# Whole gates behind every second attention chunk, and one pair of PSUM banks for two chunks' results

## The chip, the cores and the metric

The kernel runs on one core of a Trainium2 chip. The metric is the device time in microseconds (us) of one execution. TensorE (PE) multiplies matrices, VectorE (DVE) and ScalarE (ACT) work elementwise, GpSimd (POOL) works elementwise too and issues transfers, SyncE (SP) issues transfers. Matmul results land in PSUM, which has 8 banks of 2 KB per partition.

## The reference

Three layers in float32, one behind the other. First a linear attention with a decaying state, over 4 batches, 8 heads, 768 positions, head size 64; then two feed-forward layers over all 3072 tokens:

```
state = gamma * state + outer(k[t], v[t])
y[t]  = scale * q[t] @ state
x = y as (3072, 512)
x = (((x @ w1) * (x @ w2)) @ w3) @ w_out            # 512 -> 1024 -> 1024 -> 512
h = x @ w_in;  out = (h * sigmoid(1.702 h)) @ w_out2 # 512 -> 2048 -> 512
```

The five weight matrices come as 64-bit numbers.

## The kernel before

Each operand of a large product is split into a high and a low part (`wh`, `wl`, `xh`, `xl`), and a product is three matmuls: wh·xh, wh·xl, wl·xh (`mm3`, L258 to L260). One result of 128 by 512 is one bank.

**Attention** (class `Attention`, method `run`) goes over 24 chunks of 128 positions, 6 per batch. For chunk c it issues, in this order: the scores of chunk c+1 (`scores`, matmuls L379 into the tile `s`; on ACT and POOL the scaled values `vs`, L371 and L390); the part of chunk c's result that comes from the state (`across`, L434, into `y`; none in the first chunk of a batch); the masking of the scores of c+1 (`masked`, DVE L397, reads `s`); the state's update (`updates`, L410 into `u`; none in the last chunk of a batch) and its copy (`next_state`, ACT L422); the part from within the chunk (`within`, L445, into `y`); the scaled result out of `y` (`outputs`, DVE L464); the load of a later chunk's q, k and v (POOL, L360). The order is written out by hand (`manual_schedule`), and each engine takes its instructions in it. `s` is one tile of two banks. `y` is a pair of tiles of two banks each, used in turn, of which a chunk fills half of each bank.

**Between these steps** `run` calls `fill(c, at)` at four places: `at` 0 after `across`, 1 after `masked`, 2 after `within`, 3 after `outputs`. What `fill` does:

- From chunk 9 on, at 3, half a gate: the 12 matmuls of one 128 by 512 result of the first feed-forward layer's first block of 512 tokens (`first_gate`, tile `psg`, L258 to L260). Gate t has two halves, x @ w1 and x @ w2.
- At 0, what was left over from the last half (`first_out`): ACT copies the first half into `h` (L1002), or DVE multiplies `h` by the second half (L1004); after each second gate a store.
- At 1, in chunks 2 to 5 and 10 to 13, the split of an attention result into high and low parts (ACT L1018; DVE or POOL L1020).
- At 1 and 3, `work(n)`: the next n steps of the weights' preparation (`weight_steps`), as many as `PACE` says. Of a tile of weights there are ten steps on DVE: two clamps (L195), two low parts of the tile before (L149), two shifts (L203), two merges (L207), two signs (L217). Ahead of the first sign step ACT takes the magnitudes of the next tile's two pieces (L140), which wait for the transfer of the raw pieces (L130, five buffers); behind each sign step ACT casts the high part (L144). The low part of tile t is done, and gate t may be issued, with step 10 for t = 0 and step 10t + 12 behind it. All in all 86 steps belong to this stage.

Before the change, two steps went with each of chunks 5 to 8, then 7, 6, and 5 per chunk. Fifteen halves lay behind chunks 9 to 23; the sixteenth went, after attention, into a bank of `y`. The second stage (`psm`) follows: all other blocks' gates.

Of the kernel before, what the change touches and what calls it, by code (L numbers as in the profile page):

```python
# [7 lines left out]
F32 = mybir.dt.float32  # L8
# [8 lines left out]
P = 128  # L17
# [3 lines left out]
NP = H // 2  # L21
TB = 512
NB = NT // TB
CPB = TB // P
KD, KF, KG = DM // P, DF // P, DG // P
# [7 lines left out]
LEAST, MOST = 2.0, (1 + 0x680000 / 2**23) * 2.0**32  # L33
TILE_OPS = 10
PACE = dict.fromkeys(range(5, 9), (0, 2, 0, 0))
PACE.update({9: (0, 2, 0, 5), 10: (0, 1, 0, 5)})
NM = KF // 2
ORDER = (0, 2, 4, 1, 3, 5)
TOKENS = (0, 3, 1, 4, 2, 5)
# [9 lines left out]
def tile_kernel(  # L49
# [12 lines left out]
    nc = tc.nc  # L62
# [56 lines left out]
    def fetch(held=False, queue=nc.sync):  # L119

        nonlocal fetched
        if fetched >= min(used + R_BUFS, 2 * len(tiles)):
            return
        i, c = divmod(fetched, 2)
        fetched += 1
        src = tiles[i][0][:, c * WC : (c + 1) * WC].bitcast(I32)
        raw = prep.tile([P, WC, 2], I32, tag="r", bufs=R_BUFS, name="raw")
        if held:
            nc.vector.memset(raw[:, :1], 0)
        queue.dma_start(raw, src.rearrange("p (c w) -> p c w", w=2))  # L130
        raws.setdefault(i, []).append(raw)

    def magnitude(i):
        if i >= len(tiles):
            return
        xs = wx.setdefault(i, [])
        for raw in raws.get(i, [])[len(xs) :]:
            x = prep.tile([P, WC], F32, tag="x", bufs=6, name="x")
            high = raw[:, :, 1].bitcast(F32)
            nc.scalar.activation(x, high, AF.Abs, scale=2.0**16)  # L140
            xs.append(x)
# [97 lines left out]
    complete = done = 0  # L239
# [4 lines left out]
    def work(n):  # L244

        nonlocal complete, done
        for _ in range(n):
            if done < limit:
                complete = next(steps, len(tiles))
                done += 1  # L250

    def weight(i):
        while complete <= i:
            work(1)
        return parts[i]

    def mm3(ps, wh, wl, xh, xl, start, stop):
        nc.tensor.matmul(ps, wh, xh, start=start, stop=False, skip_group_check=True)  # L258
        nc.tensor.matmul(ps, wh, xl, start=False, stop=False, skip_group_check=True)  # L259
        nc.tensor.matmul(ps, wl, xh, start=False, stop=stop, skip_group_check=True)  # L260

    xhl = {}
# [23 lines left out]
    def gate_half(t, m, key, ps):  # L286

        w = [x.rearrange("p (m k f) -> p m k f", m=2, k=KD) for x in weight(t)]
        xh, xl = xhl[key]
        for d in range(KD):  # L290
            mm3(ps, w[0][:, m, d], w[1][:, m, d], xh[:, d], xl[:, d], d == 0, d == KD - 1)
# [11 lines left out]
    def h_tile():  # L303
        return xs.tile([P, 2, TB], F32, tag="h", bufs=2, name="h")
# [12 lines left out]
    qkt, kvt, dyt, pt, vs, us, ys = {}, {}, {}, {}, {}, {}, {}  # L317

    class Attention:


        def __init__(self, pool, ps):
            self.pool, self.ps = pool, ps
            self.fixed = pool.tile([P, FIXED], F32, name="fixed")
            a, b = 2 * P, 2 * P + NCK * H
            self.mask = self.fixed[:, :a].rearrange("p (n e t) -> p n e t", n=1, e=2)
            self.dv = self.fixed[:, a:b].rearrange("p (n h o) -> p n h o", n=NCK, o=1)
            self.step = self.fixed[:, b : b + NCK * KD].rearrange(
                "p (n k o) -> p n k o", n=NCK, o=1
            )  # L330
            self.state = [pool.tile([P, NP, D], F32, name=f"state{i}") for i in range(2)]
            self.s = ps.tile([P, 2, NP, P], F32, name="s")
            nc.vector.memset(self.s, 0.0)
            self.y = [ps.tile([P, 2, NP, P], F32, name=f"y{i}") for i in range(2)]

        def tile(self, kind, n, bufs):
            return self.pool.tile([P, n], F32, tag=kind, bufs=bufs, name=kind)
# [90 lines left out]
                        yield 2 * r + h, j, ys[c][h * D : (h + 1) * D, j, r]  # L428

        def across(self, c):  # L430
            ys[c] = self.y[c % 2][:, :, : NP // 2]
            for p, j, out_y in () if c % NCK == 0 else self.places(c):
                k = slice(j * D, (j + 1) * D)
                nc.tensor.matmul(  # L434
                    out_y,
                    self.state[c % 2][k, p],
                    qkt[c][k, 0, p, :],
                    start=(p < 2),
                    stop=False,
                    skip_group_check=True,  # L440
                )
# [523 lines left out]
    with tc.manual_schedule():  # L965
# [4 lines left out]
        with (  # L970
            tc.tile_pool(name="p0", bufs=1, reuse_waits="tile") as p0,
            tc.tile_pool(name="ps0", bufs=1, space=PSUM, reuse_waits="tile") as ps0,
        ):
            attention = Attention(p0, ps0)
            nc.scalar.activation(still[:, :1], still[:, :1], AF.Copy, scale=0.5)
            attention.load(0)
            nc.sync.dma_start(attention.fixed, cfix)
            attention.load(1)
            attention.factors(0)
            for c in range(2, 6):  # L980
                attention.load(c)
            for _ in range(2):
                fetch(queue=nc.gpsimd)
            attention.factors(1)
            halves = 0
            late = []
            wide = ps0.tile([P, TB], F32, name="psg")

            def first_gate(ps):
                nonlocal halves  # L990
                t, m = divmod(halves, 2)
                gate_half(t, m, 0, ps)
                late.append((t, m, ps))
                halves += 1

            def first_out(t, m, ps):
                nonlocal h
                if m == 0 and t % 2 == 0:
                    h = h_tile()
                out = h[:, t % 2]  # L1000
                if m == 0:
                    nc.scalar.copy(out, ps)  # L1002
                    return
                nc.vector.tensor_tensor(out, out, ps, ALU.mult)  # L1004
                if t % 2:
                    nc.sync.dma_start(hd[0][:, t // 2, :2], h)

            def fill(c, at):
                for _ in range((c, at) in ((6, 0), (7, 0), (8, 0))):
                    fetch(held=True)  # L1010
                if at == 3 and c > 2 * CPB and halves // 2 < min(complete, KF):
                    first_gate(wide)
                if at == 0:
                    while late:
                        first_out(*late.pop())
                if at == 1 and c in (*range(2, 6), *range(10, 14)):
                    hi, lo, x = first_x.pop(0)
                    nc.scalar.copy(hi, x)  # L1018
                    engine = nc.vector if c > 2 * CPB else nc.gpsimd
                    engine.tensor_tensor(lo, x, hi.bitcast(F32), ALU.subtract)  # L1020
                if c > CPB:
                    work(PACE.get(c, (0, 1, 0, 4))[at])
                if (c, at) == (8, 2):
                    magnitude(1)

            attention.run(fill)
            free = [
                y[:, j].rearrange("p n t -> p (n t)")
                for y in attention.y[::-1]
                for j in range(2)  # L1030
            ]
            while late:
                first_out(*late.pop())
            while halves < 2 * KF:
                weight(halves // 2)
                first_gate(free.pop(0))
                work(2)
                first_out(*late.pop())
        with (
            tc.tile_pool(name="ps1", bufs=1, space=PSUM, reuse_waits="tile") as psb,  # L1040
            ExitStack() as stage,
# [12 lines left out]
            def mix_mm(f):  # L1054
                h3, l3 = (x.rearrange("p (k f) -> p k f", k=KF) for x in weight(W3 + f))
                ps = psw if f == 0 else mixed_bank()
                for low in range(2):
                    for k in range(KF):
                        ho, lo = (
                            x.rearrange("p (k f) -> p k f", k=2)[:, k % 2]  # L1060
                            for x in weight(WO + k // 2)
                        )
                        for w, x in ((l3, ho),) if low else ((h3, ho), (h3, lo)):
                            nc.tensor.matmul(  # L1064
                                ps,
                                w[:, k],
                                x,
                                start=(k, low) == (0, 0) and x is ho,
                                stop=(k, low) == (KF - 1, 1),
                                skip_group_check=True,  # L1070
                            )
                return ps
# [45 lines left out]
            for n, i in list(enumerate(ORDER))[1:]:  # L1118
                nxt = ORDER[n + 1] if n + 1 < NB else None
                for t in range(KF):  # L1120
# [14 lines left out]
                    while rows < KF and (complete > W3 + rows or (n, t) == (2, KF - 1)):  # L1135
                        ps = mix_mm(rows)
# [162 lines left out]
```

## Time and profile before

| | |
|---|---|
| three runs, us | 964.36, 964.99, 965.16 (median 964.99) |
| the profiled execution | 965.16 us, span 963.4 us |
| granted TensorE clock | 1.000 |
| busy share of the span | PE 98%, DVE 73%, ACT 45%, POOL 24% |
| first `psg` matmul, first `psm` matmul | at 44.05 us, at 126.57 us |

The span is the time from the first to the last instruction. Starts of instructions below are in us from its beginning. A matmul's row shows its whole passage; the next one starts before it ends, so PE's time is read from start to start.

### The profile page before, as it was taken

Reading aid. Unit: us, or ns where it says so; the run is one execution under the profiler, and the core shown is the slowest. Engines: PE = TensorE matmul, PEld = TensorE weight load, DVE = VectorE, ACT = ScalarE, POOL = GpSimd, SP = SyncE. Lnnn points to the kernel's source line nnn. Section 1 sums busy time; section 2 is a strip of 40 time slices with the busy share of each in tenths; the row PEclk is TensorE's granted clock in tenths of the full one; section 3 lists DMA queues with packets and bytes.
Section 4 is the critical chain, followed back from the end, with each engine's and each line's share of the span. In section 5 each row is a group of like instructions: output and inputs, shape, how many; then the busy total and the mean of one; then the engine's idle time right before and its main releaser. Section 6 shows DMA issues by size and latency. Waiting matters only on the chain.

```text
span 963.4 us, 14665 instructions
## 1 busy us (share of the span) xinstructions
PE 946.0 (98%) x5656; PEld 781.6 (81%) x5656; DVE 707.1 (73%) x857; ACT 433.0 (45%) x643; POOL 227.3 (24%) x280
## 2 busy tenths in 40 slices
PE   6899999999999999999999999999999999999998
PEld 5787788888888888888888888888888888888886
DVE  6898878989889886766795776567486655566662
ACT  4555444433222222654536575566545544353440
POOL 6422100478687875330020000000000000000000
PEclk9999999999999999999999999999999999999999
DMA  9999765679998999899777746745987867766761
GB/s 354 374 380 354 282 213 204 217 243 356 317 367 301 354 336 403 304 321 325 260 244 272 285 175 230 299 187 202 323 316 277 327 230 260 254 216 231 272 231 54
DMA packets 90454, 268.52 MB, mean 279 GB/s; under 512 B 7248, under 2 KB 15824, under 8 KB 82320
## 3 DMA queue, kind: packets, MB, share of 16 engines
q1 hardware_dynamic: 74448, 188.74, 55.4%
q0 software_dynamic: 15792, 78.78, 21.5%
q8 instruction: 44, 0.72, 0.3%
q14 instruction: 26, 0.21, 0.1%
q10 hardware_dynamic: 144, 0.07, 0.0%
HBM read 166.37 MB, written 101.19 MB: 278 GB/s over the span
## 4 chain that ended last, share of the span: by engine, by line
PE 96%; DMA 2%; issue 1%; ACT 0%; DVE 0%; POOL 0%; DVEq 0%; POOLq 0%; ACTq 0%
PE m L258 12%; PE m L259 12%; PE m L260 12%; PE psm L259 8%; PE psm L260 8%; PE psm L258 8%; PE psw L1064 5%; PE a L258 4%; PE a L260 4%; PE a L259 4%; PE e L260 2%; PE e L259 2%; PE e L258 2%; DMA qkv<-in_qkv_dram 2%; PE y L445 2%; PE psg L258 2%
## 5 line engine op out<-in xcount | busy, mean ns | idle before, releaser
L258 PE MATMUL psm<-xh,wh 128*128 128x512 f32 x320 | 124.5, 389 | 0.0
L259 PE MATMUL psm<-xl,wh 128*128 128x512 f32 x320 | 124.5, 389 | 0.0
L260 PE MATMUL psm<-xh,wl 128*128 128x512 f32 x320 | 124.5, 389 | 0.0
L258 PE MATMUL m<-h,op 128*128 128x512 f32 x320 | 124.5, 389 | 0.0
L260 PE MATMUL m<-h,op 128*128 128x512 f32 x320 | 124.5, 389 | 0.0
L259 PE MATMUL m<-l,op 128*128 128x512 f32 x304 | 118.3, 389 | 0.0
L742 ACT CAST h<-l 128x2048 fp32r<-128x2048 f32 x38 | 72.2, 1914 | 82.0 <-PE m L260 59.0
L743 DVE TENSOR_TENSOR l<-l,h 128x2048 fp32r<-128x2048 f32 x38 | 85.4, 2285 | 17.5 <-ACT h L742 17.4
L748 POOL DMA_DIRECT2D op<-sw x6 | 3.2, 532 | 388.4 <-PE a L260 211.5
L140 ACT ACTIVATE x<-raw 128x512 f32<-128x512 f32 x72 | 47.1, 676 | 68.8 <-DMA raw<-in_wo_dram 36.6
L258 PE MATMUL a<-yh,op 128*128 128x512 f32 x192 | 74.8, 390 | 0.3 <-ACT s L614 0.3
L260 PE MATMUL a<-yh,op 128*128 128x512 f32 x192 | 74.7, 389 | 0.0
L259 PE MATMUL a<-yl,op 128*128 128x512 f32 x192 | 74.7, 389 | 0.0
L258 PEld LDWEIGHTS psm<-xh,wh 128*128 128x128 f32 x320 | 60.1, 188 | 12.6
L260 PEld LDWEIGHTS m<-h,op 128*128 128x128 f32 x320 | 60.1, 188 | 12.6
L258 PEld LDWEIGHTS m<-h,op 128*128 128x128 f32 x320 | 60.1, 188 | 12.5
L259 PEld LDWEIGHTS psm<-xl,wh 128*128 128x128 f32 x320 | 60.1, 188 | 12.5
L260 PEld LDWEIGHTS psm<-xh,wl 128*128 128x128 f32 x320 | 60.1, 188 | 12.4
L259 PEld LDWEIGHTS m<-l,op 128*128 128x128 f32 x304 | 57.1, 188 | 11.6
L258 PE MATMUL m<-h,wh 128*128 128x512 f32 x168 | 65.4, 389 | 0.0
L260 PE MATMUL m<-h,wl 128*128 128x512 f32 x168 | 65.4, 389 | 0.0
L174 DVE TENSOR_TENSOR l<-l,h 128x2048 fp32r<-128x2048 f32 x19 | 43.5, 2292 | 25.0 <-ACT h L273 23.5
(178 smaller groups left out, 2089.6 us busy)
## 6 DMA issues: line engine op xcount, KB each, us to landing
l<-gd SPq DMA_DIRECT2D x38, 1024.0 KB, 6.7
gd<-t SPq DMA_DIRECT2D x24, 1024.0 KB, 4.8
qkv<-in_qkv_dram POOLq DMA_DIRECT2D x20, 1024.0 KB, 9.3
l<-hd SPq DMA_DIRECT2D x19, 1024.0 KB, 8.1
raw<-in_w_dram SPq DMA_DIRECT2D x30, 512.0 KB, 5.9
hd<-g POOLq DMA_DIRECT2D x12, 1280.0 KB, 7.4
raw<-in_wo_dram SPq DMA_DIRECT2D x24, 512.0 KB, 7.2
gd<-g SPq DMA_DIRECT2D x24, 512.0 KB, 2.6
```

Of the source, the lines that this page charges most:

```text
L140: nc.scalar.activation(x, high, AF.Abs, scale=2.0**16)
L174: nc.vector.tensor_tensor(lo, x, hi.bitcast(F32), ALU.subtract)
L258: nc.tensor.matmul(ps, wh, xh, start=start, stop=False, skip_group_check=True)
L259: nc.tensor.matmul(ps, wh, xl, start=False, stop=False, skip_group_check=True)
L260: nc.tensor.matmul(ps, wl, xh, start=False, stop=stop, skip_group_check=True)
L445: nc.tensor.matmul(out_y, vs[c][:, 2 * p + j, :], pt[c][:, j, p, :], start=(c % NCK == 0 and p < 2), stop=True, skip_group_check=True,)
L742: nc.scalar.copy(hi, x.bitcast(F32))
L743: nc.vector.tensor_tensor(x, x.bitcast(F32), hi.bitcast(F32), ALU.subtract)
L748: queue.dma_start(t.bitcast(F32), sw[PART[name]])
L1064: nc.tensor.matmul(ps, w[:, k], x, start=(k, low) == (0, 0) and x is ho, stop=(k, low) == (KF - 1, 1), skip_group_check=True,)
```

## The change

`y` becomes one tile of two banks: even chunks use the first half of each bank, odd chunks the second. The freed bank makes `psg` a pair. `fill` issues both halves of a gate behind every odd chunk from 9 on, and none behind the even ones; within a half, all eight matmuls with wh come first, then the four with wl. `first_out` takes both halves, at 0 of the next (even) chunk. `PACE` changes with it: 9 steps with chunk 9, 4 with chunk 10, 3 with chunk 12, otherwise 8 with an odd and 2 with an even chunk. All eight gates lie within attention; the loop behind it finds nothing to do.

```
-PACE.update({9: (0, 2, 0, 5), 10: (0, 1, 0, 5)})
+PACE.update({9: (0, 2, 0, 7), 10: (0, 1, 0, 3), 12: (0, 1, 0, 2)})
...
-            self.y = [ps.tile([P, 2, NP, P], F32, name=f"y{i}") for i in range(2)]
+            self.y = ps.tile([P, 2, NP, P], F32, name="y")
...
-            ys[c] = self.y[c % 2][:, :, : NP // 2]
+            ys[c] = self.y[:, :, c % 2 * (NP // 2) :][:, :, : NP // 2]
...
-            wide = ps0.tile([P, TB], F32, name="psg")
+            wide = [ps0.tile([P, TB], F32, name=f"psg{m}") for m in range(2)]
...
-                gate_half(t, m, 0, ps)
+                wh, wl = (x.rearrange("p (m k f) -> p m k f", m=2, k=KD)[:, m] for x in weight(t))
+                xh, xl = xhl[0]
+                terms = [(w[:, d], x[:, d]) for d in range(KD) for w, x in ((wh, xh), (wh, xl))]
+                terms += [(wl[:, d], xh[:, d]) for d in range(KD)]
+                for n, (w, x) in enumerate(terms):
+                    nc.tensor.matmul(
+                        ps, w, x, start=n == 0, stop=n == len(terms) - 1, skip_group_check=True
+                    )
...
-                if at == 3 and c > 2 * CPB and halves // 2 < min(complete, KF):
-                    first_gate(wide)
+                if at == 3 and c > 2 * CPB and c % 2 and halves // 2 < min(complete, KF):
+                    for ps in wide:
+                        first_gate(ps)
                 if at == 0:
                     while late:
-                        first_out(*late.pop())
+                        first_out(*late.pop(0))
...
-                    work(PACE.get(c, (0, 1, 0, 4))[at])
+                    work(PACE.get(c, (0, 1, 0, 7 if c % 2 else 1))[at])
...
             while halves < 2 * KF:
                 weight(halves // 2)
-                first_gate(free.pop(0))
+                for ps in wide:
+                    first_gate(ps)
                 work(2)
-                first_out(*late.pop())
+                while late:
+                    first_out(*late.pop(0))
```

## Rows read from the trace of the kernel before

**Rows 1.** Stretch: length, then busy us (instructions) of each engine, clock, DMA share, GB/s.

```profile
300.00:450.00 150.00, 150.00 (x663) 124.22 (x662) 111.15 (x116) 56.31 (x68) 80.46 (x89) 1.00 0.94 340
```

**Rows 2.** PE in order of time, chunk 15: start, us, engine, line, operation, out<-in, count.

```profile
74.63 0.90 PE L379 MATMUL s<-qkv 64*64 64x128 f32 x32
75.35 0.62 PE L434 MATMUL y<-qkv,state 64*64 64x128 f32 x16
...
77.39 0.50 PE L258 MATMUL psg<-xh,wh 128*128 128x512 f32 x1
...
80.34 0.90 PE L379 MATMUL s<-qkv 64*64 64x128 f32 x32
```

**Rows 3.** PE in order of time, chunk 23 and the end of attention.

```profile
119.38 0.67 PE L434 MATMUL y<-qkv,state 64*64 64x128 f32 x16
...
121.00 0.50 PE L258 MATMUL psg<-xh,wh 128*128 128x512 f32 x1
...
123.85 0.39 PE L258 MATMUL y<-xh,wh 128*128 128x512 f32 x1
...
126.57 0.39 PE L258 MATMUL psm<-xh,wh 128*128 128x512 f32 x1
```

**Rows 4.** PE in order of time, chunk 12, the first of a batch.

```profile
57.95 0.90 PE L379 MATMUL s<-qkv 64*64 64x128 f32 x32
...
60.27 0.50 PE L258 MATMUL psg<-xh,wh 128*128 128x512 f32 x1
```

**Rows 5.** DVE in order of time, chunk 15; in brackets, idle time and its releaser.

```profile
74.74 0.69 DVE L1004 TENSOR_TENSOR h<-h,psg 128x512 f32<-128x512 f32 x1 [0.19 <-PE psg L260]
75.60 1.23 DVE L397 TENSOR_TENSOR pt<-s,fixed 128x1024 f32<-128x1024 f32 x1 [0.17 <-PE s L379]
76.74 0.68 DVE L149 TENSOR_TENSOR wl<-x,wh 128x512 fp32r<-128x512 f32 x1
77.51 0.69 DVE L464 TENSOR_TENSOR xb<-y,dy 128x512 f32<-128x512 f32 x1
78.11 0.94 DVE L203 TENSOR_SCALAR x<-x 128x512 int32<-128x512 int32 x2
```

**Rows 6.** DVE in order of time, weight steps and remainder of chunks 9 and 10.

```profile
46.28 0.75 DVE L203 TENSOR_SCALAR x<-x 128x512 int32<-128x512 int32 x2
46.95 0.68 DVE L207 SCALAR_TENSOR_TENSOR x<-raw,x 128x512 int32<-128x512 int32 x1
...
49.11 0.68 DVE L1020 TENSOR_TENSOR xl<-xb,xh 128x512 fp32r<-128x512 f32 x1
...
50.91 1.28 DVE L217 SCALAR_TENSOR_TENSOR x<-raw,x 128x512 int32<-128x512 int32 x2
52.11 0.76 DVE L195 TENSOR_SCALAR x<-x 128x512 f32<-128x512 f32 x2
```

**Rows 7.** ACT in order of time, chunks 10 and 11.

```profile
47.11 0.59 ACT L1002 COPY h<-psg 128x512 f32<-128x512 f32 x1 [0.81 <-PE psg L260]
...
49.06 0.37 ACT L422 COPY state<-u 128x256 f32<-128x256 f32 x1 [0.84 <-PE u L410]
...
50.44 0.67 ACT L140 ACTIVATE x<-raw 128x512 f32<-128x512 f32 x1 [0.42 <-DMA raw<-in_w_dram]
51.63 1.22 ACT L144 CAST wh<-x 128x512 fp32r<-128x512 f32 x2 [0.53 <-DVE x L217]
52.76 1.06 ACT L371 ACTIVATE vs<-qkv,fixed 128x64 f32<-128x64 f32 x4
```

**Rows 8.** PE in order of time, chunks 7 to 9: two stalls and the first gate.

```profile
35.36 0.39 PE L410 MATMUL u<-vs,qkv 128*64 128x64 f32 x6 [0.72 <-issue]
...
41.75 0.34 PE L379 MATMUL s<-qkv 64*64 64x64 f32 x4 [1.62 <-issue]
...
44.05 0.50 PE L258 MATMUL psg<-xh,wh 128*128 128x512 f32 x1
```

**Rows 9.** Loads of q, k, v from 40 to 130 us, by tile.

```profile
DMA to landing us min/median/max: 7.6/8.7/10.6
```

More of the change, by code (lines that the diff above doesn't have):

```diff
@@ L1026, in tile_kernel @@
             attention.run(fill)
[L1027 to L1031, printed above, removed]
             while late:
-                first_out(*late.pop())
+                first_out(*late.pop(0))
             while halves < 2 * KF:
                 weight(halves // 2)
-                first_gate(free.pop(0))
+                for ps in wide:
+                    first_gate(ps)
                 work(2)
-                first_out(*late.pop())
+                while late:
+                    first_out(*late.pop(0))
         with (
```

## The prediction

> **What bounds the kernel now.** I read the busy times by stretch first. From 300 to 450 us TensorE (PE) is busy 150.00 of 150.00 us [rows 1], and it looks like this from the end of attention nearly to the last instruction. So whatever attention gains or loses reaches the end whole: nothing later can absorb it. Then the order of time on PE. A chunk with half a gate behind it runs from scores at 74.63 to the gate at 77.39 (2.76 us) and from there to the next scores at 80.34 (2.95 us) with no gap [rows 2]: PE is its own limit here. The question is whether the engines that PE waits for, VectorE (DVE) and ScalarE (ACT), still keep up in the new order; so I read their order of time [rows 5 to 7].
>
> Chunk c on PE: scores(c+1), across(c), updates(c), within(c). On DVE: the pending gate product (L1004), mask(c+1) (L397), in chunks 10 to 13 a remainder (L1020), one weight step, y out (L464, "ship"), the other weight steps. On ACT: vs(c+1) (L371), the gate copy (L1002), in those chunks a cast (L1018), the state copy (L422), then what the weight steps bring: magnitudes (L140) and casts (L144). Each engine takes its instructions in this order.
>
> **The gain.** Twelve gate matmuls cost 2.95 us between attention matmuls [rows 2], 2.85 (121.00 to 123.85) with attention only ahead, and 2.72 (123.85 to 126.57) between gates [rows 3]. A pair costs 2.95 + 2.72 = 5.67. Before, 15 halves stand alone and the 16th follows the 15th; after, there are 8 pairs. Seven seams of 0.23 go: 1.6 us. The number of matmuls stays. The order within a gate (the wl products last) and the weight steps (86 by the end in both) move no work in or out: 0.
>
> **The waits that come.** Without a half gate behind every chunk, an even chunk gives DVE and ACT 2.76 us where they had 5.71. Three things can end too late.
>
> (1) y. One pair of banks holds two chunks, so across(c+1) writes where ship(c) reads. In the trace of before, the two used different tiles; a write beside a read in one bank is not shown. Bounds: 0, or the whole of ship. I take the whole, as scores and mask, which share one tile, also never overlap. Ship starts 0.12 after the PE step that follows within (77.51 against 77.39) and lasts 0.69 [rows 2, 5], so it ends 0.81 into scores; across would start at 0.72 (75.35 - 74.63). With 0.05 from DVE to PE that is 0.13 per even chunk, if DVE is free. Chunk 18 has no across of its own and its scores-to-gate time is 2.32 (57.95 to 60.27) [rows 4]; DVE is then late: mask starts 0.97 after scores (75.60 - 74.63), the next step 1.14 later, ship 0.60 after that [rows 2, 5]; ship ends at 3.39, across is due at 3.04: 0.40. Behind chunk 22 no scores remain to cover it: ship ends 0.85 after within. Odd chunks have the gate as cover: 0. Chunks 0 to 8: ship ends late by at most some 0.6 in sum, but PE stands still there anyway, 0.72 at 35.36 and 1.62 at 41.75, for nothing that the profile shows [rows 8]; I take 0, with 0.6 as the other end. Here the trace has no row, and a page has a rule: the Trainium skill ("PSUM — Partial Sum Buffer", section "PSUM bank collisions raise a hardware error") has software keep PE writes and DVE reads apart by bank, whatever the address. By it these waits are due; without it the sum falls to that of rival C.
>
> (2) ACT, once. Chunk 9 now takes seven weight steps instead of five (9 to 17 in place of 15). The 17th brings the magnitudes of the third weight tile and a cast. The second magnitude waits for its transfer: it starts at 50.44, released by the DMA, in the run before [rows 7]. That transfer was issued in chunk 8, which the change leaves alone, so I take 50.44 again. Before, this stood behind chunk 10's copies; now everything of chunk 10 on ACT stands behind it: 50.44 + 0.67, cast 0.61, vs 1.06, copy 0.59 [rows 7], less some 0.25 where neighbours overlap: the first copy ends at 53.1. DVE's product needs it, and mask(11) is behind the product.
> PE: gate(9) 44.05 [rows 8] + 5.67 = 49.72 scores(11); due then are scores(12) at 52.48 and across(11) at 53.20.
> DVE: product 53.1 to 53.8 (0.60 from start to start, as all steps here), mask 1.14 [rows 5], remainder 0.60, L217 0.60 [rows 6] to 56.1, ship to 56.8. Scores(12) has to wait for mask: 55.05 instead of 52.48. ACT's second cast follows that L217 (56.2 + 0.6), then the state copy 0.37 [rows 7]: 57.2, the later of the two that across(11) needs. Loss 57.2 - 53.2 = 4.0.
>
> (3) DVE's backlog after it. Gate(11) starts 1.62 after across (as 119.38 to 121.00 [rows 3]; neither has updates) at 58.8, scores(13) follows at 64.45. DVE from 56.7: two L195 0.67, L149 0.60, mask 1.14, remainder 0.60, L149 0.60, ship 0.60: 60.9; L203 twice 0.67, L207 and L217 twice 1.2 each [rows 5, 6]: 64.0. Cast 64.6, vs 65.6, gate copy 66.2 on ACT. So the product runs 66.2 to 66.8 though the gate's matmuls ended at 64.6; mask 67.95, remainder, one L195, ship: 69.6. Scores(14) is due at 64.45 + 2.32 = 66.77 and gets mask at 68.05; across(13) is due at 67.49 and starts at 69.65. Loss 2.15. The same once more for scores(15) at 77.35: DVE is through with its L217s at 76.1, the gate copy at 78.3, the product at 78.95, mask 80.1, L149, ship 81.4; across(15) was due at 77.35 + 2.76 + 0.72 = 80.83. Loss 0.6. From chunk 16 on DVE has caught up: its last L217 is done 3.5 us into the gate, and cast, vs and copy (2.2) fit before its end at 5.67.
>
> Sum: 4.0 + 2.15 + 0.6 + 0.13 (chunk 16) + 0.40 (18) + 0.13 (20) + 0.85 (22) = 8.25; less 1.6: +6.65. The profiled execution took 965.16 us (span 963.4 and 1.76 around it), 0.17 above the median of the runs. Forecast 965.16 + 6.65 = 971.8 us.
>
> SP and POOL: the q/k/v loads (POOL) of even chunks are issued some 11.2 us before use instead of 17; their landing takes 7.6 to 10.6 us [rows 9], so 0, but with little left. The raw loads (SP) keep their two chunks of lead.
>
> **Rivals.**
> A (46%): as above, 971.8, its own range 970.5 to 973.
> B (14%): the raw piece lands 3 us earlier, or ACT's order is kinder; then (2) costs only the bank wait behind DVE's load in chunk 10, 0.6. 965.16 + 8.25 - 4.0 + 0.6 - 1.6 = 968.4. For it: transfers share busy queues. Against: nothing ahead of that transfer changes.
> C (8%): the halves of y are independent. Across(11) still waits for state (4.0); (3) shrinks to scores(14) behind mask, 1.3, and 0.1; the rest goes. 965.16 + 5.4 - 1.6 = 969.0. For it: no row shows such a wait.
> D (14%), not slower: the gate copy leaves ACT before its pair is done in every chunk, as I have it from chunk 16 on. Then mask always starts 0.97 after scores and only bank waits stay: 0.6 (chunk 10), 0.75 (12), 0.13 three times (14, 16, 20), 0.40, 0.85: 3.0 - 1.6 = +1.4, 966.5. It decides from where ACT's magnitude starts before 47.0, that is 2.2 + 0.5 ahead of scores(11) at 49.72, instead of 50.44, and the casts of chunk 11 as much ahead of scores(13). Against it: 50.44.
> E (10%): D and C together, the seams alone: 965.16 - 1.6 = 963.6; a little more per seam (0.3) gives 963.0.
> F (8%): A and more. Chunks 0 to 8 don't absorb their 0.6, or stalls without a cause, as at 35.36 and 41.75 (0.7 to 1.6 [rows 8]), come back in the gateless chunks, where 160 small matmuls follow each other: +0.6 to +3.2, 972.4 to 975.
>
> **How the numbers follow.** The time is A's, 971.8. The range of 8 in 10 leaves out E and the upper part of F: 966.3 to 973.4. What a measurement tells from no change is 0.2%, 1.93 us: 963.06 to 966.92. Faster: the outer part of E, 6%. Within: D and the rest of E, 18%. Slower: A, B, C, F, 76%.
>
> **What would show it.** In the changed trace: pairs of gates of 5.67 us (the gain). PE idle some 2.5 us ahead of the scores behind chunk 10's within, released by mask, with ACT's L140 at about 50.4 released by the raw transfer and the gate copy near 53 (2). Again some 1.3 us ahead of scores(14) (3). Across released by DVE's ship in even chunks, 0.1 to 0.4, and 0.85 ahead of the last across (1). First psm matmul at 133 instead of 126.57, and from there the same 150.00 of 150.00. I am wrong if L140 isn't held at 50.4, if mask starts 0.97 after scores in chunks 10 and 12, or if across starts while ship reads.

## The result, and the profile after

The changed kernel takes 974.77 us (median of four runs, 973.38 to 975.84) against 964.90 (964.36 to 965.16): 1.0102 times the time, 95% interval 1.0085 to 1.0120. It is slower, as forecast, but by 9.9 us where 6.7 were forecast, and above the range, which ended at 973.4. The profiled execution took 975.84 us (span 974.0, granted clock 0.999); the first `psg` matmul stands at 44.11 us, the first `psm` matmul at 134.91 (before: 44.05 and 126.57). In this kernel the gate matmul is L997, the copy L1009, the product L1011, cast and remainder L1026 and L1028.

The stretch from the first gate to the end of attention holds most of the loss. One row for it: length, then busy us (instructions) of PE, PEld, DVE, ACT and POOL, clock, DMA share, GB/s; with it the stretch of [rows 1], which is as full as it was.

```profile
44.00:135.00 91.00, 82.83 (x1205) 67.37 (x1202) 72.53 (x117) 40.57 (x105) 14.98 (x24) 1.00 0.83 296
...
300.00:450.00 150.00, 150.00 (x663) 123.91 (x661) 114.28 (x117) 54.34 (x69) 85.06 (x95) 1.00 0.93 335
```

PE has the same 83 us of work as before and 8.2 us without any; the granted clock is 1.00, so the loss is waiting. The waits of PE in this stretch, by what ended them (us in total, times, longest):

```profile
PE s L379 <- DVE pt L397: 3.8, 3, 1.9
PE y L434 <- DVE xb L464: 3.0, 4, 1.1
PE y L434 <- DVE x L195: 1.2, 1, 1.2
```

The first line is scores waiting for the mask, the second across waiting for ship. PE in order of time shows where (these answer to [rows 2 to 4]):

```profile
44.11 0.50 PE L997 MATMUL psg<-xh,wh 128*128 128x512 f32 x1
...
49.79 0.90 PE L379 MATMUL s<-qkv 64*64 64x128 f32 x32
...
54.49 0.90 PE L379 MATMUL s<-qkv 64*64 64x128 f32 x32 [1.87 <-DVE pt L397]
56.61 0.67 PE L434 MATMUL y<-qkv,state 64*64 64x128 f32 x16 [1.22 <-DVE x L195]
...
63.90 0.90 PE L379 MATMUL s<-qkv 64*64 64x128 f32 x32
...
67.97 0.90 PE L379 MATMUL s<-qkv 64*64 64x128 f32 x32 [1.68 <-DVE pt L397]
69.60 0.67 PE L434 MATMUL y<-qkv,state 64*64 64x128 f32 x16 [0.73 <-DVE xb L464]
...
77.37 0.90 PE L379 MATMUL s<-qkv 64*64 64x128 f32 x32
...
80.47 0.90 PE L379 MATMUL s<-qkv 64*64 64x128 f32 x32 [0.28 <-DVE pt L397]
82.47 0.67 PE L434 MATMUL y<-qkv,state 64*64 64x128 f32 x16 [1.09 <-DVE xb L464]
...
104.77 0.67 PE L434 MATMUL y<-qkv,state 64*64 64x128 f32 x16 [0.32 <-DVE xb L464]
...
127.72 0.67 PE L434 MATMUL y<-qkv,state 64*64 64x128 f32 x16 [0.89 <-DVE xb L464]
...
134.91 0.39 PE L258 MATMUL psm<-xh,wh 128*128 128x512 f32 x1
```

The rows at 54.49, 67.97 and 80.47 are scores(12), (14) and (16), which wait for the mask of the chunk before; those at 56.61, 69.60 and 82.47 are across(11), (13) and (15), the last two waiting for ship of chunks 12 and 14; across(19) and across(23), at 104.77 and 127.72, wait for ship of chunks 18 and 22. At 56.61 the row names DVE's L195, which is not what across needs: ACT's state copy, at 56.19 to 56.55, came last.

ACT at chunk 10 (answers to [rows 7]): the second magnitude waits 3.06 us for the raw transfer, and the cast, the four `vs` and the gate copy stand behind it.

```profile
49.96 0.68 ACT L140 ACTIVATE x<-raw 128x512 f32<-128x512 f32 x1 [3.06 <-DMA raw<-in_w_dram]
50.54 0.60 ACT L144 CAST wh<-x 128x512 fp32r<-128x512 f32 x1
51.05 1.06 ACT L371 ACTIVATE vs<-qkv,fixed 128x64 f32<-128x64 f32 x4
52.02 0.56 ACT L1009 COPY h<-psg 128x512 f32<-128x512 f32 x1
```

DVE then gets the product only when that copy is through (answers to [rows 5, 6]); the last three lines are chunk 14's:

```profile
52.61 0.69 DVE L1011 TENSOR_TENSOR h<-h,psg 128x512 f32<-128x512 f32 x1 [3.73 <-ACT h L1009]
53.22 1.22 DVE L397 TENSOR_TENSOR pt<-s,fixed 128x1024 f32<-128x1024 f32 x1
...
58.56 1.14 DVE L1028 TENSOR_TENSOR xl<-xb,xh 128x512 fp32r<-128x512 f32 x1
...
79.20 1.22 DVE L397 TENSOR_TENSOR pt<-s,fixed 128x1024 f32<-128x1024 f32 x1
80.34 1.38 DVE L149 TENSOR_TENSOR wl<-x,wh 128x512 fp32r<-128x512 f32 x1
81.64 0.68 DVE L464 TENSOR_TENSOR xb<-y,dy 128x512 f32<-128x512 f32 x1
```

### The profile page after: what moved, and what is told of

It is laid out like the page before. It is cut to its first block, busy times and chain, and to the rows that moved or that the text cites. A ratio compares the mean times of both kernels' runs of the same rounds, so it can differ in the third digit from the quotient of the medians.

```text
span 974.0 us, 14681 instructions
## 1 busy us (share of the span) xinstructions
PE 948.7 (97%) x5656; PEld 783.5 (80%) x5656; DVE 705.7 (72%) x857; ACT 431.8 (44%) x643; POOL 225.6 (23%) x280
## 4 chain that ended last, share of the span: by engine, by line
PE 86%; DMA 5%; DVE 4%; ACT 2%; issue 1%; SPq 0%; POOL 0%; ACTq 0%; DVEq 0%; POOLq 0%
PE m L259 11%; PE m L258 11%; PE m L260 11%; PE psm L259 7%; PE psm L260 7%; PE psm L258 7%; PE psw L1069 4%; PE a L258 4%; PE a L259 4%; PE a L260 4%; PE psg L997 2%; DMA qkv<-in_qkv_dram 2%; PE e L258 2%; PE e L259 2%; PE e L260 2%; DMA l<-hd 1%
```

## The experiments

Theory 1 is the prediction's: ACT's order (a magnitude that waits, then the gate copy) holds DVE's mask, and the shared banks add a wait of across for ship. Theory 2: the shared banks alone make the loss. Theory 3: the gateless chunks cost PE more by themselves.

Theory 3 falls by the changed kernel's own rows. Chunk 16 has no gate and PE waits for nothing in it; from its scores to the next it takes 2.76 us, as from scores to gate in [rows 2].

```profile
90.22 0.90 PE L379 MATMUL s<-qkv 64*64 64x128 f32 x32
...
92.98 0.90 PE L379 MATMUL s<-qkv 64*64 64x128 f32 x32
```

### Step 17 in chunk 10 instead of 9

```diff
-PACE.update({9: (0, 2, 0, 7), 10: (0, 1, 0, 3), 12: (0, 1, 0, 2)})
+PACE.update({9: (0, 2, 0, 6), 10: (0, 1, 0, 4), 12: (0, 1, 0, 2)})
```

> The changed kernel with one weight step moved from chunk 9 to chunk 10 (6 and 5 steps instead of 7 and 4), so that ACT meets the magnitude that waits for the raw transfer behind chunk 10's gate copy. Theory 1 (ACT's queue holds the gate copy, the copy holds the product, the product holds the mask): no PE wait for the mask ahead of scores(12), across(11) about 54.2 instead of 56.6 us, 2.5 us less than the changed kernel, about 972.3. Rival (the shared banks of y are the cost, across waiting for the result's read-out): ACT's order does not matter, 974.8 within 0.6.

Measured: 971.72 us (971.18 to 972.22), ratio 1.0066 (1.0049 to 1.0082). The copy stands in front of the magnitudes again, and the wait of scores(12) is gone; across(11) waits 0.71 for the state, and the second pair of waits is as it was:

```profile
55.00 0.67 PE L434 MATMUL y<-qkv,state 64*64 64x128 f32 x16 [0.71 <-ACT state L422]
66.51 0.90 PE L379 MATMUL s<-qkv 64*64 64x128 f32 x32 [1.80 <-DVE pt L397]
68.13 0.67 PE L434 MATMUL y<-qkv,state 64*64 64x128 f32 x16 [0.73 <-DVE xb L464]
```

Moving one step by one chunk gave back 3.1 us, though no bank and no gate changed. That is the price of step (2).

### The first half copied right behind its gate

```diff
                     for ps in wide:
                         first_gate(ps)
+                    first_out(*late.pop(0))
```

> The changed kernel with ACT's copy of a gate's first half issued right behind the gate, ahead of that chunk's casts and magnitudes and of the next chunk's scaled values. Theory 1: the product finds its copy done at the end of each gate; the waits for the mask ahead of scores(12), (14) and (16) go (1.9, 1.7 and 0.3 us), those of across(11), (13) and (15) shrink; some 5 us less than the changed kernel, about 969.8. Rival (shared banks of y): unchanged, 974.8 within 0.6.

Measured: 970.43 us, ratio 1.0053 (1.0036 to 1.0069). The copy now starts when the gate's first half ends (47.06), ahead of everything that chunk 9's steps bring. No scores wait for a mask any more; what waits is across, for the held state copy and for ship:

```profile
55.60 0.98 PE L434 MATMUL y<-qkv,state 64*64 64x128 f32 x16 [2.27 <-DVE x L195]
56.51 1.97 PE L445 MATMUL y<-pt,vs 128*64 128x128 f32 x16
...
68.82 0.67 PE L434 MATMUL y<-qkv,state 64*64 64x128 f32 x16 [1.17 <-DVE xb L464]
```

All mask waits came from the copy's place in ACT's queue, those of chunk 12 too. The long rows at 55.60 and 56.51 are PE at a lower clock, some 1.5 us of this profile (last section).

### Both together

> Both edits of the two runs before this one together, on the changed kernel. Theory 1: only the waits for the shared banks stay (about 0.7 in chunks 10 and 12, 0.15 to 0.3 in 14, 16 and 20, 0.5 in 18, 0.95 in 22: 3 to 3.5 us) against 1.5 us gained by the seams; 966.5 to 968. Rival (shared banks are all of it): 974 or more.

Measured: 969.12 us (968.54 to 971.05), ratio 1.0041 (1.0027 to 1.0056); a miss by about 1. PE's waits between first gate and first `psm`:

```profile
PE y L434 <- DVE xb L464: 2.6, 3, 1.4
PE y L434 <- ACT state L422: 0.7, 1, 0.7
```

With ACT's order out of the way 5.7 us are back, and 85.90 us lie between first gate and first `psm`, against 82.52 before. Most of what is left is across waiting for ship, above all behind DVE's load in chunk 12 (1.41). The waits, 3.3 us, are twice what the seams give (1.5); a seam is the 0.2 us by which a half gate between attention matmuls is dearer than one behind another half.

### The shared banks alone, in the kernel before

```diff
-            self.y = [ps.tile([P, 2, NP, P], F32, name=f"y{i}") for i in range(2)]
+            self.y = ps.tile([P, 2, NP, P], F32, name="y")
...
-            ys[c] = self.y[c % 2][:, :, : NP // 2]
+            ys[c] = self.y[:, :, c % 2 * (NP // 2) :][:, :, : NP // 2]
...
+            free = [attention.y[:, j].rearrange("p n t -> p (n t)") for j in range(2)]
```

> The kernel before with nothing but the shared y: one tile of two banks, half gates behind every chunk as before. Theory 1: behind a half gate the result has long been read when the next across starts, and in chunks 0 to 8 the stalls for instructions and loads absorb it; 964.9 within 0.7. Rival (shared banks are the cost): across waits in all 24 chunks, 2 us or more above the kernel before.

Measured, in ten runs: 966.74 us, ratio 1.0016 (1.0006 to 1.0025): 1.9 us slower where none was expected. Its PE waits up to the first `psm`:

```profile
PE psm L258 <- DVE h L1004: 0.8, 1, 0.8
...
PE y L434 <- DVE xb L464: 0.5, 1, 0.5
```

The 0.8 is a by-product: with two banks of `y` fewer, the sixteenth half sits in a bank that the first `psm` needs, and its product is still reading there. The one wait for ship listed, 0.5, lies ahead of the first gate, which still starts at 43.16; from there on, with a half gate behind each chunk, no across waits for ship. The rest of the 1.9 us is not placed. Theory 2 falls: it would need 9.9, and across waits for ship in this stretch only together with gateless chunks.

### The same kernel again

> The changed kernel again, unaltered, to see whether what it lost behind attention comes back (from the first psm matmul to the end its profile took 839.1 us, the kernel before and e1 to e4 836.8 to 837.0). Theory 1: it was of that execution; 836.9 again, and 973.6 in all. Rival (the change shifts the loads of the later stages so that they come late): 839 again, 974.8 or more.

Measured: 975.01 us (974.41 to 975.84), ratio 1.0100 (1.0087 to 1.0113); the profiled execution 974.41. The waits stand at the same places within 0.2 us (2.06, 1.22, 1.68, 0.72, 0.30, 1.06, 0.31, 0.89), first gate to first `psm` takes 90.97 us, and from there to the end 837.00. In the first profile of the changed kernel that last part was 839.14, before the change 836.78: the 2.4 us that the first profile lost late belong to that execution, not to the change. The median did not come back with them: 973.6 was expected, 975.01 came.

### The state's update ahead of across

The aim was to give ship more time: `updates` and `next_state` stand before `across`, and the weight steps of even chunks behind ship, on top of the kernel with both edits.

```diff
-PACE.update({9: (0, 2, 0, 6), 10: (0, 1, 0, 4), 12: (0, 1, 0, 2)})
+PACE.update({9: (0, 2, 0, 6), 10: (0, 0, 0, 5), 12: (0, 0, 0, 3)})
...
+                self.updates(c)
+                self.next_state(c)
                 self.across(c)
...
-                self.updates(c)
-                self.next_state(c)
                 self.within(c)
...
-                    work(PACE.get(c, (0, 1, 0, 7 if c % 2 else 1))[at])
+                    work(PACE.get(c, (0, 1, 0, 7) if c % 2 else (0, 0, 0, 2))[at])
```

> The kernel of e4 with the state's update and copy issued ahead of across, and with the weight step of even chunks behind the read-out of y instead of ahead of it. Theory 1, as mended by e1 to e4 (what is left in e4 is across waiting for the read-out, 0.25 to 1.4 us a time): the update covers the read-out, all waits of across go but some 0.2 in chunk 11 and 0.95 ahead of the last across; about 964.6, 4.5 us less than e4. Rival (the waits for y are set by something other than the read-out's place, transfers or ACT): less than 2 us gained on e4, 967 or more.

Measured: 970.20 us, ratio 1.0051 (1.0037 to 1.0065). The waits for ship in chunks 14 to 20 went, but the time didn't fall: 964.6 was expected. So the order alone was put into the kernel before:

> The kernel before with nothing changed but the order of one chunk's PE work: the state's update (and its copy) ahead of across instead of behind it. It asks why e5 gained nothing. Theory 1, as mended by e5 (PE pays at each change of the operands' shape: scores and across have the same, update and within have the same, and an update put between scores and across makes two more changes, 0.31 us per chunk in e5's trace): 10 of the 15 chunks with gates have both steps, 3.1 us, 968.0. Rival (e5's loss came from its own weight steps and waits): 965.0 within 0.7.

Measured: 969.12 us, ratio 1.0042 (1.0030 to 1.0054). Chunk by chunk, with nothing waited for:

```profile
69.70 0.90 PE L379 MATMUL s<-qkv 64*64 64x128 f32 x32
70.53 0.69 PE L410 MATMUL u<-vs,qkv 128*64 128x64 f32 x16
71.14 0.67 PE L434 MATMUL y<-qkv,state 64*64 64x128 f32 x16
71.74 1.09 PE L445 MATMUL y<-pt,vs 128*64 128x128 f32 x16
72.77 0.50 PE L258 MATMUL psg<-xh,wh 128*128 128x512 f32 x1
```

Scores to gate takes 3.07 us here and 2.76 in [rows 2], with the same 80 matmuls. Scores and across have operands of one shape (64*64), updates and within of another (128*64); the new order alternates between them and costs 0.31 per chunk. In the ten chunks that have both steps this is 3.1 of the 4.3 us lost; the rest is not placed. That the change of shape is the cause is argued from these rows, not tried by itself.

### The last gate in halves, the remainders on POOL

Four kernels, with the weight steps of even chunks behind ship in all (but one of chunk 22's two, and chunk 21 takes one more): the last gate in halves behind chunks 22 and 23, with the update first or in its old place, each without and with the remainders of chunks 10 to 13 on POOL.

```diff
-PACE.update({9: (0, 2, 0, 6), 10: (0, 0, 0, 5), 12: (0, 0, 0, 3)})
+PACE.update({9: (0, 2, 0, 6), 10: (0, 0, 0, 5), 12: (0, 0, 0, 3), 21: (0, 1, 0, 8), 22: (0, 1, 0, 1)})
...
+                if at == 3 and c >= NC - 2 and halves // 2 < min(complete, KF):
+                    first_gate(wide[halves % 2])
-                if at == 3 and c > 2 * CPB and c % 2 and halves // 2 < min(complete, KF):
+                elif at == 3 and c > 2 * CPB and c % 2 and halves // 2 < min(complete, KF):
...
-                    engine = nc.vector if c > 2 * CPB else nc.gpsimd
+                    engine = nc.gpsimd
```

Update first, DVE keeps the remainders, then POOL has them:

> e5 with the last gate in halves behind chunks 22 and 23, the remainders left on DVE. Theory 1: 0.95 us of wait goes, 0.2 of a seam comes back; 963.9. It tells the two edits of e6 apart.

> e5 with two more edits: the remainders of chunks 10 to 13 on POOL instead of DVE, and the last gate again in halves, one behind chunk 22 and one behind chunk 23, so that the last across has a cover. Theory 1: only seams are left, 6 of 7 gained, 963.7; at most 1.4 us under the kernel before. Rival: POOL, which shares SBUF with DVE, is late with the remainders or slows DVE's weight steps; 965 or more.

Update in its old place, the same pair:

> The kernel of e4 (across in its old place) with the weight step of even chunks behind the read-out of y, and the last gate in halves behind chunks 22 and 23. Theory 1: across still waits for the read-out 0.24 us in each gateless chunk, 0.8 in chunk 13; the wait ahead of the last across is gone; from first psg to first psm matmul 83.4 us against 82.5 of the kernel before and 85.9 of e4; 966.2. What the seams give (0.21 a pair) and what the shared banks take (0.24 a pair) then nearly cancel, and no order of the other engines' work makes the change a gain. Rival (DVE's and ACT's queues were the whole loss): 963.5 to 964.

> e10 with the remainders of chunks 10 to 13 on POOL. Theory 1: the wait in chunk 13 falls from 0.8 to 0.2 as DVE has one step less ahead of the read-out; 965.7. Rival (POOL is late, or slows DVE): 966.2 or more.

Measured, in this order: 969.43, 970.58, 970.01 and 968.82 us (ratios 1.0043, 1.0060, 1.0047 and 1.0040, the intervals all between 1.0028 and 1.0074). All four missed. The wait of 0.9 ahead of the last across is gone in all, at the price of a seam. POOL gained nothing clear (970.58 for 969.43, 968.82 for 970.01), and DVE's own steps got longer beside it. DVE, then POOL, of the last kernel, where the remainder is L1031:

```profile
57.47 1.72 DVE L149 TENSOR_TENSOR wl<-x,wh 128x512 fp32r<-128x512 f32 x1
...
66.55 4.01 DVE L149 TENSOR_TENSOR wl<-x,wh 128x512 fp32r<-128x512 f32 x2
```

```profile
57.35 1.28 POOL L1031 TENSOR_TENSOR xl<-xb,xh 128x512 fp32r<-128x512 f32 x1 [3.38 <-ACT xh L1029]
...
67.49 1.29 POOL L1031 TENSOR_TENSOR xl<-xb,xh 128x512 fp32r<-128x512 f32 x1
...
69.32 0.70 POOL L390 TENSOR_TENSOR vs<-qkv,fixed 128x256 f32<-128x256 f32 x1
```

A low part (L149) takes 0.68 us alone. The first ends 0.56 after POOL's remainder (59.19 and 58.63), the second two 0.54 after POOL's last step (70.56 and 70.02). The mean of L149 in this stretch rises from 702 ns to 910 where the remainders moved to POOL with the update first, from 765 to 914 with the update in its place.

## Why the prediction was wrong

The side, the kind of wait and the places were right. What failed is step (3), which gave POOL's steps no effect on DVE's; smaller terms were short too. Lateness per place, from start to start on PE:

| | forecast | measured |
|---|---|---|
| (2) across(11) | 4.0 | 3.34 (due 53.27, at 56.61) |
| (3) across(13) | 2.15 | 2.66 (due 66.94, at 69.60) |
| (3) across(15) | 0.6 | 1.62 (due 80.85, at 82.47) |
| (1) chunks 16, 18, 20, 22 | 0.13, 0.40, 0.13, 0.85 | 0.24, 0.50, 0.23, 0.96 |
| seven seams | -1.6 | -1.5 (a pair 5.68, 44.11 to 49.79) |
| sum | +6.65 | +8.0 |

First gate to first `psm` grew by 8.28 us in fact (90.80 against 82.52), and by 8.45 in the second profile. The missing 0.3 lies in across itself: where it comes late it takes 0.60 from its start to the next step, otherwise 0.55.

**The gain** was right: 0.22 per seam for 0.23.

**Step (2)** was right. The magnitude started at 49.96 (forecast 50.44) and the copy ended at 52.58 (53.1); the run with step 17 a chunk later shows the price. With the magnitude moved, 971.7 came out, with the copy always in time 970.4, with both 969.1. Rival B put the first of these cases at 968.4, rival D the others at 966.5. B's own step was near (3.4 us for the measured 3.1); its sum was low as A's was. D was low since across(13) still waits 1.41 for ship behind DVE's load in chunk 12, where D's sum has 0.75.

**Step (3)** is the one that failed. It laid DVE's steps end to end at the lengths of [rows 5, 6], treated POOL as a queue of loads and gave its `vs` no effect on DVE. Three of DVE's steps met a `vs` and took 0.46, 0.43 and 0.70 us longer; in its two places step (3) was 0.51 and 1.02 short. Across(13) came at 69.60, forecast 69.65, but by luck: what step (2) had too much (0.66), this had too little (0.51), and 0.46 of that is the remainder at 58.56, which took 1.06 from start to start instead of 0.60. Across(15) came at 82.47 instead of 81.4. Of these 1.07 us, 0.25 came with the mask (79.20 for 78.95), behind a shift at 72.30 that took 0.76 from start to start instead of 0.33; 0.10 from ship's end to across (82.32 to 82.47, for 0.05); and 0.70 from one low part that took 1.30 from start to start, where I had put the 0.60 of [rows 5]. POOL's `vs` falls elsewhere in this order than before:

```profile
58.51 0.62 POOL L390 TENSOR_TENSOR vs<-qkv,fixed 128x256 f32<-128x256 f32 x1
...
72.09 0.76 POOL L390 TENSOR_TENSOR vs<-qkv,fixed 128x256 f32<-128x256 f32 x1
...
80.53 0.63 POOL L390 TENSOR_TENSOR vs<-qkv,fixed 128x256 f32<-128x256 f32 x1
```

```profile
72.30 0.84 DVE L203 TENSOR_SCALAR x<-x 128x512 int32<-128x512 int32 x1
```

DVE's remainder at 58.56 ended at 59.70, 0.57 after the first; the shift ended 0.29 after the second; the low part at 80.34 ended at 81.72, 0.56 after the third. In the second profile the three took 1.13, 0.84 and 1.36 at the same places. Each time DVE's step runs about as if it began when POOL's ended, as in the two runs with POOL's remainders. A step that reads PSUM was not held: the mask at 53.22 kept its 1.22 beside a `vs` at 52.95. The trace of before had such a meeting: two shifts take 0.94 in [rows 5] and 0.75 in [rows 6], and beside the first stands

```profile
77.79 0.63 POOL L390 TENSOR_TENSOR vs<-qkv,fixed 128x256 f32<-128x256 f32 x1
```

The Trainium skill has the rule ("SBUF — State Buffer", section "SBUF: two separate sides"): VectorE and GpSimd share a pair of ports that one of them holds for a whole instruction, and a DVE step with two SBUF inputs is shut out by it. The rows of the remainder and the low part agree. The section gives the pair to the one that starts first; that the rows do not bear out, as the low part's starts 0.19 before POOL's. The shift has one SBUF input, and no row says why it was held too. No run took `vs` out of the way, so this part is read from rows and not tried.

**Step (1)** was right in kind: across waits for ship in every gateless chunk, never where a gate stands between, and the independent halves of rivals C and E are out. Every term was some 0.1 short. I took 0.05 from DVE's end to PE's start; the rows show 0.15 to 0.16 (ship ends at 69.44 and 82.32, across starts at 69.60 and 82.47).

**What followed attention** was right: 836.78 us before, 837.00 in the second profile, and the first profile's 2.4 more did not come back. That chunks 0 to 8 absorb their part is not shown: the first gate started at 44.11, and at 43.16 with the shared banks alone, but among all profiles anywhere from 42.62 to 45.57 us, which hides 0.6. Rival F's number (972.4 to 975) fits, but the stalls without a cause that its upper part counts on are not there: every wait of PE in the stretch has a releaser.

**What stays open.** The forecast of the first `psm` was 133.2, it came at 134.91: 1.7 of the 3.0 us between forecast and median. The other 1.3 are not placed. The first gate's start varies by more than that. And the mean granted clock was 0.998 or less in 6 of the 8 runs of the changed kernel, in 8 of 37 runs of the kernel before beside the experiments; there those 8 took 966.5 to 967.1 us, the rest 963.9 to 966.0. Whether the changed kernel's median holds such a part was not separated: its two profiled executions ran at 0.999 and 1.000, and that at 1.000 took 974.41.

## What to carry to other kernels

Merging work into fewer, larger blocks saves a seam (0.2 us here) and takes away the cover under which other engines finished every second time; price each shortened stretch by the slowest engine's queue in order, including what stands in front of a copy there. When steps move, place every neighbour's steps anew, POOL's too: a DVE step on SBUF operands that met one was 0.4 to 1.0 us longer here. A resource that is shared without cost under cover costs a wait where the cover goes.

## What the runs showed that was not expected

PE's clock fell after waits. In the kernel with the last gate split and the update in its old place, scores and across waited 1.69 and 1.30 us, and these are the stretches there (columns as in the first fence):

```profile
66.00:68.00 2.00, 0.70 (x34) 0.57 (x26) 1.45 (x3) 2.00 (x8) 0.00 (x0) 1.00 0.84 244
68.00:70.00 2.00, 2.00 (x36) 1.67 (x38) 2.00 (x4) 0.31 (x2) 0.00 (x0) 0.59 1.00 369
70.00:72.00 2.00, 2.00 (x18) 1.63 (x15) 1.80 (x4) 0.32 (x1) 0.89 (x2) 0.56 0.97 394
72.00:74.00 2.00, 2.00 (x10) 1.65 (x9) 2.00 (x5) 0.00 (x0) 0.31 (x1) 1.00 1.08 397
```

After the waits, from 68 to 72 us, the engine ran mostly at the lower of its two levels (1.2 GHz), though it had work throughout. The two runs of that kernel with a mean clock of 1.000 took 967.66 and 968.08 us, the four with 0.998 or 0.996 took 969.55 to 972.73. Two more profiles have it. With the copy early, behind the wait of 2.27 us, the granted clock is 0.50 from 56 to 58 us and 0.69 from 58 to 60, and within takes 1.90 us (56.51 to 58.41) for 1.02 elsewhere. With the update first and POOL's remainders, behind a wait of 1.76, it is 0.59 and 0.56 from 66 to 70. So the time behind a wait on PE can cost more than the wait's length; what decides it these runs don't tell, as in the changed kernel's two profiles waits of 1.87 and 2.06 us, each with one of 1.22 behind it, left the clock at 1.00.

The other two are above: a DVE step on SBUF operands that meets one of POOL's takes 0.4 to 1.0 us longer, and another order of the same 80 matmuls costs PE 0.31 us per chunk.
